# A new hand-written order for window attention with routed experts: all pieces re-ordered, sums and scores split in two float32r parts, masks loaded first, fewer idle products

## The chip, the cores and the metric

The program runs on one core of one Trainium2 chip. The number that counts is the device time of one execution in microseconds (us); lower is better. A core has five engines that run in parallel, each through its own list of instructions and strictly in that list's order: TensorE (PE, matrix products), VectorE (DVE), ScalarE (ACT), GpSimd (POOL) and SyncE (SP, which here only issues DMAs). They wait for each other through semaphores.

## The reference

Eight batches, each with eight attention heads over 576 positions and a head size of 64. Four heads look at a plain window of 32 positions, four at 32 positions with a step of 4. The attention result (576 x 512 per batch) goes through a routed expert: the 128 rows of each batch with the highest score get a two-layer product added.

```
scores = q @ k.T / 8                       # per batch and head, 576 x 576, masked to the window
attn   = softmax(scores)
x      = (attn @ v), heads side by side    # 8 x 576 x 512, float32
score  = x @ w_gate                        # 8 x 576
top    = the 128 rows of each batch with the highest score
out    = x, but out[top] = x[top] + sigmoid(score[top]) * (relu(x[top] @ w1) @ w2)
# w1: 512 x 1024, w2: 1024 x 512
```

## The kernel before, in words

**Pieces and their order.** The work is cut into some 1,100 pieces, and a table, `ORDER`, lists them. The program goes through the table once and issues the instructions of each piece on the engines that it uses, so the table fixes the order on every engine's list and in the DMA queues; there is no scheduler behind it. A piece is a letter code with its indices, `S 1 4` for batch 1, unit 4.

**Attention.** Each batch has five units `u` (0 and 1 hold the stepped heads, 2 and 3 the plain ones, 4 the rest of both). A unit runs through these pieces:
- `Q`, `K`, `VL`: DMAs that load queries, keys and values, nearly all on SP's queue. `ZP`, `ZV`, `ZA` spread loaded queries into a padded tile on POOL, DVE or ACT.
- `S` (lines 353 and 360): scores on PE; first a product of an identity with the mask tile `mk`, then 32 small products. `MX` (L367): row maximum on DVE. Then either `SU` (subtract on DVE) or `CS` (copy on ACT) and `SP2` (subtract on POOL).
- `TR` (L386): transposes on PE. `EX` (L395, L399): exponentials on ACT. `V` (L414): product with the values on PE.
- `DN`: divisors on DVE. `XM` (DVE, L435) or `XA` (ACT): the division. `ST`: store to the output by DMA.
- The gate score: either `GD` (product and sum on DVE, L471) or `GM` (product on POOL) and `GA` (sum on ACT).

**Routing, once a batch.** `RX` (`split_sums`, L481 to L492) splits six gate sums into three bfloat16 parts and spreads them by `blk`; `RO` (`in_order`, L502 and L504) brings them into row order by products on PE with the selection tiles `selw` and `sel_l`; `SC` adds the parts; `TP` splits the score into three bfloat16 parts on POOL; `SP` and `SB` make a row of it; `RK` (L530) and `RC` (L538) count the rank of each row; `RA`, `MV` (DVE) or `MK` (POOL) mark the rows with rank below 128; `PK` (L558) picks index and score by products; `IX`, `SG`, `SH` finish them, and `GT` gathers the 128 rows by an indirect DMA on POOL. `RO` and `PK` are exact because the parts add up to the float32 value.

**Experts.** `XT`, `XH`, `XL` turn the gathered rows and split them in a high and a low float32r part. Batches 1 and 2, 3 and 4, 5 and 6 share the first layer (`F`, L638, with `HH`, `HL`); batches 0 and 7 go alone (`N`, L654, `RL`, `HT`, `HI`, `HO`). `Y` (L679) is the second layer, `YO` (L684) the result and `SY` (L689) the indirect DMA that writes it back. There are 128 pieces `F`, `N` and `Y`, of six or three products each. The weights come by `LW` (DMA on SP's queue, two buffers), `WH` or `WV` (high part), `WL` (low part on POOL, which frees the buffer).

**The rest.** `C` pieces build constants: `C 0` issues the DMAs of the masks (`mraw`) and of the identity (`id32`) on POOL's queue, and `C 1` makes the bfloat16 identity `id16` (L191) and the first mask tile from them. `W n` (`idle`, L697) issues n products whose result nobody reads, so that PE has something to do; the program opens with `WARM` = 9 of them.

## Time and profile before

| | |
|---|---|
| device time, median of 3 runs | 284.77 us (283.71 to 286.86) |
| the profiled execution | 284.33 us, span 282.6 us |
| PE busy | 246.6 us, 87% of the span |
| DVE busy | 180.4 us, 64% |
| ACT busy | 146.2 us, 52% |
| POOL busy | 157.5 us, 56% |
| mean granted TensorE clock | 0.963 of full speed |
| moved by DMA | 53.15 MB |

The profiled execution is one run; its own time is 1.7 us longer than the span of its instructions. PE's busy time holds idle products and products at half clock too, so its 87% is more than the share of useful work.

### The profile page before, as it was taken

Reading aid. Unit: us, or ns where it says so; the run is one execution under the profiler, and the core shown is the slowest. Engines: PE = TensorE matmul, PEld = TensorE weight load, DVE = VectorE, ACT = ScalarE, POOL = GpSimd, SP = SyncE. Lnnn points to the kernel's source line nnn. Section 1 sums busy time; section 2 is a strip of 40 time slices with the busy share of each in tenths; the row PEclk is TensorE's granted clock in tenths of the full one; section 3 lists DMA queues with packets and bytes.
Section 4 is the critical chain, followed back from the end, with each engine's and each line's share of the span. In section 5 each row is a group of like instructions: output and inputs, shape, how many; then the busy total and the mean of one; then the engine's idle time right before and its main releaser. Section 6 shows DMA issues by size and latency. Waiting matters only on the chain.

```text
span 282.6 us, 8986 instructions
## 1 busy us (share of the span) xinstructions
PE 246.6 (87%) x3623; PEld 212.3 (75%) x3623; DVE 180.4 (64%) x491; ACT 146.2 (52%) x412; POOL 157.5 (56%) x206
## 2 busy tenths in 40 slices
...
GB/s 244 395 272 279 273 296 335 282 218 274 343 262 155 213 294 228 220 106 360 259 244 231 144 204 96 241 196 96 179 160 118 37 2 79 70 2 0 0 74 37
DMA packets 22489, 53.15 MB, mean 188 GB/s; under 512 B 2688, under 2 KB 13184, under 8 KB 21424
## 3 DMA queue, kind: packets, MB, share of 16 engines
...
## 4 chain that ended last, share of the span: by engine, by line
PE 38%; DVE 26%; issue 20%; DMA 6%; ACT 4%; POOL 3%; POOLq 1%; SPq 0%; DVEq 0%; ACTq 0%
PE a L414 9%; PE m L638 7%; PE s L360 6%; DVE rm L530 5%; PE m L679 5%; DVE junk L471 4%; PE m L386 3%; PE m L697 2%; DVE x L435 2%; DMA vl<-in_vb_dram 2%; DVE mx L367 2%; DMA id<-in_ident_dram 2%; PE s L353 2%; DVE rx L492 2%; DMA out_dram<-x 2%
## 5 line engine op out<-in xcount | busy, mean ns | idle before, releaser
L414 PEld LDWEIGHTS a<-v,pt 128*64 128x64 f32 x1152 | 42.8, 144 | 8.4 <-issue 5.7
L414 PE MATMUL a<-v,pt 128*64 128x65 f32 x1152 | 47.7, 230 | 1.5 <-DVE x L435 1.0
L360 PEld LDWEIGHTS s<-kq,zq 128*64 128x64 f32 x1216 | 44.7, 146 | 5.0 <-issue 2.2
L360 PE MATMUL s<-kq,zq 128*64 128x64 f32 (+2 forms) x1216 | 45.2, 230 | 1.4 <-issue 1.4
L463 POOL TENSOR_TENSOR gm<-x,wg 128x512 f32<-128x512 f32 x27 | 36.2, 1341 | 17.5 <-DVE x L435 5.4
L399 ACT ACTIVATE pt<-m 64x512 f32<-64x512 f32 x48 | 28.4, 592 | 24.3 <-PE a L414 12.4
L379 POOL TENSOR_TENSOR dt<-dt,mx 128x512 f32<-128x512 f32 x20 | 22.4, 1120 | 24.6 <-ACT dt L374 16.2
L367 DVE TENSOR_REDUCE mx<-s 128x8 f32<-128x512 f32 x40 | 27.0, 679 | 12.3 <-PE s L360 8.8
L395 ACT ACTIVATE pt<-m 32x256 f32<-32x256 f32 (+1 forms) x80 | 30.0, 375 | 9.0 <-PE m L386 8.1
L530 DVE SCALAR_TENSOR_TENSOR rm<-sb,ts,thr 128x576 bf16<-128x576 f32 (+3 forms) x32 | 29.1, 949 | 6.6 <-ACT sb L523 6.6
L307 POOL COPY zq<-kq 64x1152 f32<-64x1152 f32 (+1 forms) x25 | 30.2, 1209 | 4.0 <-DMA xe<-out_dram,ix 2.5
L689 POOL DMA_INDIRECT out_dram<-y,ix x8 | 8.0, 1001 | 39.9 <-DVE y L684 35.6
L638 PE MATMUL m<-xh,w1h 128*128 128x256 f32 x96 | 29.2, 304 | 0.7 <-ACT xh L620 0.7
L638 PE MATMUL m<-xl,w1h 128*128 128x256 f32 x96 | 27.8, 290 | 0.2 <-DVE xl L623 0.2
L638 PE MATMUL m<-xh,w1l 128*128 128x256 f32 x96 | 27.7, 289 | 0.0
L386 PE MATMUL m<-id,dt 128*128 128x128 f32 x160 | 25.6, 289 | 2.0 <-DVE dt L379 1.0
L679 PE MATMUL m<-w2h,hh 128*128 128x512 f32 x64 | 27.1, 423 | 0.0
L475 ACT ACTIVATE gm<-gm 128x256 f32<-128x256 f32 x54 | 22.2, 417 | 8.5 <-POOL gm L463 8.3
L679 PE MATMUL m<-w2h,hl 128*128 128x512 f32 x64 | 25.4, 396 | 0.0
L679 PE MATMUL m<-w2l,hh 128*128 128x512 f32 x64 | 25.3, 396 | 0.0
L353 PE MATMUL s<-mk,id 128*64 128x512 bf16 x80 | 16.4, 405 | 9.5 <-DVE mk L194 6.1
L433 ACT ACTIVATE x<-a,rin 128x64 f32<-128x64 f32 x88 | 19.2, 328 | 7.1 <-DVE rin L424 5.4
...
## 6 DMA issues: line engine op xcount, KB each, us to landing
...
raw<-in_w_dram SPq DMA_DIRECT2D x8, 512.0 KB, 6.2
...
```

The source lines that it names most:

```text
L307: copy(zqs[kind][r, :, lo:hi, h], src[r, :, G * lo:G * hi].rearrange("p g (t q) -> p g t q", q=G))
L360: nc.tensor.matmul(st[HB * g:HB * (g + 1), i, lo:hi], zqs[kind][:, g, t].rearrange("p h q -> p (h q)"), ks[b, kind][:, g, k0 + lo:k0 + hi] ...
L367: nc.vector.tensor_reduce(out=mx, in_=X["s", b, u], axis=AX.X, op=ALU.max)
L379: eng.tensor_tensor(out=dt, in0=st if eng is nc.vector else dt, in1=mx.unsqueeze(2).to_broadcast([P, 8, GK]), op=ALU.subtract)
L386: nc.tensor.transpose(tt[:, a * P:(a + 1) * P], dt[:, 2 * a:2 * a + 2].rearrange("p e k -> p (e k)"), id32)
L395: nc.scalar.activation(pt[o:o + n, y, e], tt[lo:lo + n, x].rearrange("k c (i q) -> k c i q", q=G), AF.Exp, scale=SCALE)
L399: nc.scalar.activation(pt[r, :, e], tt[r].rearrange("k (i q) -> k i q", q=G), AF.Exp, scale=SCALE)
L414: nc.tensor.matmul(av[r, a // 2, f], pt[:, i % 2, i // 2, a], values(b, u, a)[:, f], start=True, stop=True)
L463: nc.gpsimd.tensor_tensor(out=gm, in0=X["x", b, u], in1=gate_w(u), op=ALU.mult)
L530: nc.vector.scalar_tensor_tensor(out=out, in0=X["sb", b][:, t * P:S], scalar=ts[:, b, t:t + 1], in1=thr[:, 0:n], op0=ALU.subtract, op1=ALU ...
L638: nc.tensor.matmul(out, WS1[w][:, i, f * P:(f + 1) * P], X["x" + x, e][:, i, :], start=i == 0 and n == 0, stop=i == 3 and n == 2)
L679: nc.tensor.matmul(X["py", b], X["h" + x, e, c][:, o:o + P], WS2[w][:, i, :], start=i == 0 and k == 0, stop=i == 7 and k == 2)
```

## The change

**The table.** All pieces stand in a new order. The choice of engine changes with it: 27 units instead of 20 subtract on POOL (`CS`, `SP2`), 13 instead of 20 on DVE (`SU`); 21 gate sums instead of 13 run on DVE (`GD`), 19 instead of 27 on POOL and ACT (`GM`, `GA`); 36 divisions instead of 29 on DVE (`XM`), 4 instead of 11 on ACT (`XA`); 18 spreads of queries instead of 25 on POOL, 10 instead of 5 on ACT, 6 instead of 4 on DVE; 7 high parts of weights instead of 4 on ACT, 1 instead of 4 on DVE; 6 marks instead of 4 on DVE, 2 instead of 4 on POOL. The pairs of batches are the same.

**Splits.** `RX` makes two float32r parts instead of three bfloat16 parts: three DVE instructions a batch instead of eight. `TP` becomes two POOL instructions instead of four. The selection tiles and the marks become float32r, so `RO` (6 products a batch) and `PK` (5) run on float32r operands.

**Start.** The mask's DMA moves to ACT's queue, ahead of all else there; `id32` follows later on the same queue (`C 16`); `id16` is built on POOL without `id32`. The first scores are those of units 2 and 3.

**Idle products.** `W` issues 30 instead of 86, `WARM` 18 instead of 9.

```diff
-BUFS = dict(v0=1, v1=1, s=2, a=1, m=4, dt=2, x=3, gm=2, xe=3, xh=1, hh=3, raw=2, y=2, oh=1, sb=1, xl=1, hl=3, mx=3, den=3, rin=3, rx=2, g=8, ix=8, junkv=1, p3=2, rest=2, sm=2, restp=2)
-WARM = 9
+BUFS = dict(v0=1, v1=1, s=2, a=1, m=4, dt=2, x=3, gm=1, xe=3, xh=1, hh=3, raw=2, y=2, oh=1, sb=1, mx=4, rx=2, xl=1, hl=3, den=4, rin=4, g=8, ix=8, p2=2, sm=1)
+WARM = 18
...
-ZP 0 0 0, S 0 0, W 26, K 0 1 1, ZP 0 0 1, MX 0 0, CS 0 0, Q 0 1 1, C 14, C 2, Q 1 0, SP2 0 0, C 4, TR 0 0, VL 0 2,
...
+Q 1 1, K 1 1, VL 0 0, S 0 2, S 0 3, C 14, ZV 0 1 0 0, ZA 0 1 1 0, CS 0 2, C 13, DT 0 3, C 6, MX 0 2, MX 0 3, S 0 0,
...
-            nc.gpsimd.dma_start(out=mraw, in_=masks)
-            nc.gpsimd.dma_start(out=id32, in_=ident)
+            nc.scalar.dma_start(out=mraw, in_=masks)
...
-            nc.vector.memset(id16, 0.0)
+            nc.gpsimd.memset(id16, 0.0)
+            for h in range(2):
+                v = id16[0:G, G * h:G * (h + 1)]
+                nc.gpsimd.affine_select(out=v, in_=v, pattern=[[1, G]], compare_op=ALU.not_equal, fill=1.0, base=0, channel_multiplier=-1)
         elif i == 1:
-            nc.vector.tensor_copy(id16[0:G], id32[0:G, 0:G].unsqueeze(1).to_broadcast([G, 2, G]))
...
+        elif i == 16:
+            nc.scalar.dma_start(out=id32, in_=ident)
...
-        nc.sync.dma_start(out=qs[b, kind][:, :, lo:hi], in_=qt[b, kind].rearrange("p (h s) -> p h s", h=2)[:, :, lo:hi])
+        (nc.scalar if b == 0 and kind else nc.sync).dma_start(out=qs[b, kind][:, :, lo:hi], in_=qt[b, kind].rearrange("p (h s) -> p h s", h=2)[:, :, lo:hi])
...
-        (nc.scalar if b == 0 else nc.sync).dma_start(out=ks[b, kind][:, :, lo:hi], in_=kt[b, kind].rearrange("p (h s) -> p h s", h=2)[:, :, lo:hi])
+        nc.sync.dma_start(out=ks[b, kind][:, :, lo:hi], in_=kt[b, kind].rearrange("p (h s) -> p h s", h=2)[:, :, lo:hi])
...
-    def three(eng, out, x, rest):
-        eng.tensor_copy(out[0], x)
-        eng.tensor_tensor(out=rest, in0=x, in1=out[0], op=ALU.subtract)
-        eng.tensor_copy(out[1], rest)
-        eng.tensor_tensor(out=out[2], in0=rest, in1=out[1], op=ALU.subtract)
+    def two(eng, hi, lo, x):
+        eng.tensor_copy(hi, x)
+        eng.tensor_tensor(out=lo, in0=x, in1=hi.bitcast(F32), op=ALU.subtract)
 
 
     def split_sums(b):
-        X["p3", b] = p3 = new("p3", [P, 3, 6], f"p3_{b}", BF16)
-        X["rx", b] = rx = new("rx", [P, 4, 3, 4], f"rx_{b}", BF16)
-        three(nc.vector, [p3[:, i] for i in range(3)], gs[:, b, 0:6], new("rest", [P, 6], f"rest_{b}"))
+        X["p2", b] = p2 = new("p2", [P, 6, 2], f"p2_{b}", F32R)
+        X["rx", b] = rx = new("rx", [P, 4, 4, 2], f"rx_{b}", F32R)
+        two(nc.vector, p2[:, :, 0], p2[:, :, 1], gs[:, b, 0:6])
+        nc.vector.tensor_tensor(out=rx, in0=p2.bitcast(F32)[:, 0:4].unsqueeze(2).to_broadcast([P, 4, 4, 2]),
+                                in1=blk.unsqueeze(1).unsqueeze(3).to_broadcast([P, 4, 4, 2]), op=ALU.mult)
...
-        three(nc.gpsimd, [tk[:, b, :, 2 + i] for i in range(3)], ts[:, b], new("restp", [P, NTOK], f"restp_{b}"))
+        two(nc.gpsimd, tk[:, b, :, 2], tk[:, b, :, 3], ts[:, b])
...
-        X["oh", b] = oh = new("oh", [P, NTOK, P], f"oh_{b}_{s}", BF16)
+        X["oh", b] = oh = new("oh", [P, NTOK, P], f"oh_{b}_{s}", F32R)
...
-            nc.tensor.matmul(pi[:, 0:5], oh[:, t, :], tk[:, b, t, :], start=t == 0, stop=t == NTOK - 1)
+            nc.tensor.matmul(pi[:, 0:4], oh[:, t, :], tk[:, b, t, :], start=t == 0, stop=t == NTOK - 1)
```

**What the table moves, at three places.** First PE at the routing of batch 1. `a` is the result of `V`, `s` that of `S`, `m` a PSUM bank; before, the last rows ahead of `RO 1` on PE and `RO 1` itself:

```order
L386 MATMUL m_66<-id_75,dt_71 128x128 x4
L414 MATMUL a_1_1125<-v_0_844,pt_99 64x65 x16
L386 MATMUL m_67<-id_75,dt_70 128x128 x4
L617 MATMUL m_68<-id_75,xe_0_973 128x128 x4
L386 MATMUL m_69<-id_75,dt_71 128x128 x4
L414 MATMUL a_0_1178<-v_0_844,pt_98 64x65 x16
L502 LDWEIGHTS selw
L502 MATMUL m_66<-rx_1197,selw 128x3x4
```

The same engine and place with the change:

```order
L420 MATMUL a_2_951<-v_1_661,pt_99 64x65 x16
L699 LDWEIGHTS warm
L699 MATMUL m_67<-warm 128x256
L359 MATMUL s_3_990<-mk,id_76 64x512
L366 MATMUL s_3_990<-kq_90,zq_88 64x64 x16
L392 MATMUL m_69<-id_75,dt_71 128x128 x4
L619 MATMUL m_67<-id_75,xe_0_939 128x128 x4
L420 MATMUL a_3_1019<-v_1_661,pt_99 64x65 x16
L504 MATMUL m_68<-rx_984,selr 128x8 x4
L506 MATMUL m_68<-p_1_983,selr 128x2 x2
```

`RO 1` stood right behind the product that came before `RX 1` in the table (nothing of PE's lies between `RX 1` and `RO 1`); now a score unit of batch 1, a turn, the turn of the gathered rows and a `V` of batch 1 stand between the two.

Second DVE at the same routing, `RX 1`. `p` are the parts, `rx` the spread parts; before:

```order
L481 CAST p_1_1196<-gs 128x6
L482 TENSOR_TENSOR rest_1198<-gs,p_1_1196 128x6
L483 CAST p_1_1196<-rest_1198 128x6
L484 TENSOR_TENSOR p_1_1196<-rest_1198,p_1_1196 128x6
L492 TENSOR_TENSOR rx_1197<-p_1_1196,blk 128x12 x4
L423 TENSOR_SCALAR den_0_1221<-a_0_1178 128x8
```

And with the change:

```order
L604 CAST w1h<-raw_805 128x1024
L487 CAST p_1_983<-gs 128x6
L488 TENSOR_TENSOR p_1_983<-gs,p_1_983 128x6
L495 TENSOR_TENSOR rx_984<-p_1_983,blk 128x32
L625 TENSOR_TENSOR xl_1014<-m_67,xh_1013 128x4x128
```

Eight instructions became three, with one that reads `blk` instead of four.

Third DVE at the start of the program, where the first masks are made. `zq` are spread queries, `kq` loaded ones, `mk` the mask tiles; before:

```order
L189 MEMSET id_76 128x32
L191 CAST id_76<-id_75 32x64
L181 COPY mk<-mraw 128x512
L194 MEMSET mk 128x2x32
L181 COPY mk<-mraw 128x512
L198 MEMSET mk 128x32
L181 COPY mk<-mraw 128x512
L307 COPY zq_90<-kq_91 64x2x8x32
```

And with the change:

```order
L184 COPY mk<-mraw 128x512
L198 MEMSET mk 128x2x32
L313 COPY zq_88<-kq_90 64x36x32
L184 COPY mk<-mraw 128x512
L204 MEMSET mk 128x32
L184 COPY mk<-mraw 128x512
L313 COPY zq_89<-kq_92 64x2x8x32
L266 TENSOR_REDUCE blk<-id_75 128x4
L373 TENSOR_REDUCE mx_2_255<-s_2_194 128x8
```

The copy from `id_75` (`id32`) no longer stands ahead of the masks; the first read of `id_75` on DVE now stands behind them and ahead of the first row maximum.

## Rows read from the trace of the kernel before

**Rows 1.** The page, part 1: busy time, share and instructions of each engine.

```profile
PE 246.6 (87%) x3623; PEld 212.3 (75%) x3623; DVE 180.4 (64%) x491; ACT 146.2 (52%) x412; POOL 157.5 (56%) x206
```

**Rows 2.** Busy by stretch: length, PE, PEld, DVE, ACT, POOL, granted clock, DMA share, GB/s.

```profile
0.00:9.30 9.30, 2.11 (x11) 1.33 (x11) 4.06 (x9) 4.19 (x5) 8.03 (x15) 1.00 0.77 287
9.30:37.50 28.20, 25.68 (x470) 21.90 (x470) 13.53 (x33) 15.64 (x43) 19.34 (x49) 1.00 0.87 298
37.50:125.00 87.50, 71.14 (x1252) 60.55 (x1251) 76.19 (x190) 52.51 (x145) 63.26 (x60) 0.90 0.76 247
125.00:217.70 92.70, 89.99 (x1557) 79.12 (x1555) 69.22 (x218) 63.10 (x196) 52.58 (x64) 1.00 0.62 198
217.70:277.20 59.50, 57.63 (x342) 49.39 (x340) 16.66 (x43) 10.75 (x25) 13.32 (x21) 0.97 0.09 32
277.20:282.60 5.40, 0.00 (x0) 0.00 (x0) 0.75 (x1) 0.00 (x0) 0.96 (x1) 0.94 0.13 49
```

**Rows 3.** The same view of the stretches with a low granted clock.

```profile
45.00:50.00 5.00, 3.45 (x43) 2.97 (x43) 3.43 (x11) 1.79 (x5) 2.55 (x6) 0.66 0.96 363
75.00:82.50 7.50, 5.38 (x106) 4.95 (x106) 5.39 (x18) 2.17 (x4) 2.83 (x6) 0.77 0.86 288
92.50:100.00 7.50, 6.07 (x91) 5.12 (x92) 7.22 (x27) 4.91 (x9) 3.78 (x4) 0.77 0.69 247
102.50:110.00 7.50, 6.90 (x116) 6.38 (x117) 5.38 (x14) 3.76 (x13) 4.33 (x8) 0.77 0.83 263
120.00:125.00 5.00, 3.90 (x44) 3.26 (x44) 3.77 (x16) 3.95 (x11) 4.48 (x7) 0.66 0.19 63
240.00:245.00 5.00, 4.78 (x28) 4.63 (x27) 0.32 (x1) 0.00 (x0) 0.72 (x1) 0.66 0.30 105
```

**Rows 4.** Waits: who waited for whom, total us, times, longest us.

```profile
PE m L502 <- DVE rx L492: 7.8, 4, 3.3
...
PE s L353 <- DVE mk L194: 6.1, 1, 6.1
...
PE m L538 <- DVE rm L530: 2.5, 4, 1.0
```

**Rows 5.** Timeline of `RX 1` and `RO 1`: start, duration, instruction, idle before.

```profile
73.62 2.34 POOL L606 TENSOR_TENSOR w2l<-raw,w2h 128x1024 fp32r<-128x1024 f32 x1
...
73.71 2.52 DVE L492 TENSOR_TENSOR rx<-p,blk 128x12 bf16<-128x12 bf16 x4
...
76.04 0.41 PE L502 MATMUL m<-rx,selw 128*128 128x12 bf16 x4 [3.30 <-DVE rx L492]
```

**Rows 6.** The chain of waits: start, us on the chain, what.

```profile
12.82 4.37 PE m L697 x26
17.18 0.44 PE m L386 x4
...
29.41 2.40 PE m L697 x22
...
185.28 2.80 PE m L679 x12
```

**Rows 7.** Timeline of the start.

```profile
7.88 0.97 DVE L191 CAST id<-id 32x64 bf16<-32x64 f32 x1 [3.63 <-DMA id<-in_ident_dram]
...
9.29 0.64 PE L353 MATMUL s<-mk,id 128*64 128x512 bf16 x2 [6.07 <-DVE mk L194]
```

**Rows 8.** Idle products (L697) and gate sums on DVE (L471): min/median/max ns, first and last start.

```profile
L697 PE MATMUL m<-warm x95: 269/273/422, 1.1 to 64.4; 128*128 128x256 bf16 x95
...
L471 DVE CUSTOM_DVE_ANT_0 junk<-x,wg x26: 414/426/1848, 38.4 to 212.9; 128x256 bf16<-128x256 f32 x26
```

**Rows 9.** DMA issues of the weights: count, KB each, median us to landing.

```profile
raw<-in_w_dram SPq DMA_DIRECT2D x8, 512.0 KB, 6.2
```

**Rows 10.** Timeline of PE late in the program.

```profile
216.58 1.15 PE L414 MATMUL a<-v,pt 128*64 128x65 f32 x32
...
229.66 0.39 PE L538 MATMUL m<-neg,rm 128*128 128x1 bf16 x10
```

More of the change, by code (lines that the diff above doesn't have):

```diff
@@ L144, in tile_window_attention_moe @@
     id32 = cp.tile([P, P], F32, name="id32")
-    id16 = cp.tile([P, 2, G], BF16, name="id16")
-    mraw = cp.tile([P, 2 * GK], BF16, name="mraw")
+    id16 = cp.tile([P, 2 * G], BF16, name="id16")
+    mraw = new("hl", [P, 512], "mraw", F32R).bitcast(BF16)[:, 0:2 * GK]
     mk = cp.tile([P, 4, 8, GK], BF16, name="mk")
     wg = cp.tile([P, 3, 256], F32, name="wg")
-    selw = cp.tile([P, P + 3], BF16, name="selw")
-    sel_l = cp.tile([P, 2, P], BF16, name="sel_l")
+    selr = cp.tile([P, 2 * (P + 2) + 2 * P], F32R, name="selr")
+    selw, sel_l = selr[:, 0:2 * (P + 2)].rearrange("p (c m) -> p c m", c=2), selr[:, 2 * (P + 2):].rearrange("p (c m) -> p c m", c=2)
     blk = cp.tile([P, 4], F32, name="blk")
@@ L167, in tile_window_attention_moe @@
     ts = cp.tile([P, B, NTOK], F32, name="ts")
-    tk = cp.tile([P, B, NTOK, 5], BF16, name="tk")
+    tk = cp.tile([P, B, NTOK, 4], F32R, name="tk")
+    tk32 = cp.tile([P, NTOK, 2], F32, name="tk32")
     gs = cp.tile([P, B, 11], F32, name="gs")
@@ L173, in tile_window_attention_moe @@
     warm = cp.tile([P, 256], BF16, name="warm")
+    X = {}
     def clear_q():
@@ L224, in constants @@
         elif i == 4:
-            nc.gpsimd.tensor_copy(tk[:, :, :, 0], toks32[:, 0:1].unsqueeze(2).to_broadcast([P, B, NTOK]))
-            for t in range(NTOK):
-                nc.gpsimd.memset(tk[:, :, t, 1], float(t * P))
+            nc.gpsimd.tensor_copy(tk32[:, :, 0], toks32[:, 0:1].to_broadcast([P, NTOK]))
+            nc.gpsimd.tensor_tensor(out=tk32[:, :, 1], in0=toks32, in1=tk32[:, :, 0], op=ALU.subtract)
+            nc.gpsimd.tensor_copy(tk[:, :, :, 0:2], tk32.unsqueeze(1).to_broadcast([P, B, NTOK, 2]))
             nc.gpsimd.memset(gs[:, :, 10], 0.0)
```

170 lines of the change are left out of this document (83 added, 87 removed).

## The prediction

> **What bounds the kernel now.** I read the busy table first [rows 1]: PE has 87% of the span, the next engine (DVE) 64%. So the question is what PE's time is made of, and when it stands still. By stretch [rows 2] there are three regimes. Up to 9.3 us nothing useful runs on PE. From 37.5 to 125 us PE is busy 71.14 of 87.5 us while DVE is busy 76.19, and the granted clock is 0.90: here PE waits for chains that run through DVE. From 125 us on PE is busy 97% and all else has slack, until the last 5.4 us, in which only the last result is written. So time is to be won before 125 us and in what PE does there; work that is merely moved within the last 150 us wins nothing.
>
> I split the span of 282.6 us into six parts, all seen from PE:
> - A, until the first useful product: 9.3 us [rows 7].
> - B, after the last product: 5.4 us [rows 2].
> - C, waits in between: PE is idle for 282.6 - 246.6 = 36.0 us; of this 5.4 lie at the end, and of the first 9.3 us 2.1 are busy, so 7.2 lie in A. C is 23.4 us. 7.8 of it are four waits of `RO` for `RX`, 2.5 four waits of `RC` for `RK` [rows 4].
> - D, idle products inside: `W` issues 86. The 26 near the start took 4.37 us (168 ns each, some at half rate), 22 later ones 2.40 (109 ns each) [rows 6]; the other 38 at 109 ns make 4.1. D is 10.9 us.
> - E, loss to the clock: six stretches [rows 3] in which a part ran at 1.2 instead of 2.4 GHz, each behind waits of PE. (1 - 0.66) x 5.0 or (1 - 0.77) x 7.5 is 1.7 us each time. E is 10.2 us.
> - F, the rest, useful work at the clock of the rest of the run: 282.6 - 59.2 = 223.4 us.
>
> **The change, part by part.**
>
> *Start.* Today the first score waits 6.07 us for the mask tile, and that for `id32`, whose copy DVE awaits for 3.63 us until 7.88 [rows 7]. With the change neither stands ahead of the first score; what does is the landing of `Q 0 0` and `K 0 0`, 2 x 576 KB. In A the DMA engines moved 287 GB/s on average [rows 2], nothing in the first two microseconds; these two and the 0.4 MB on the other queues then need until about 7 us, a spread and two mask copies on DVE about 1.5. I take A = 8.5, with 7.5 and 11 as ends (11 if loads land as slowly as the median weight load, 6.2 us [rows 9], one behind the other in part). More counts what follows: today PE fills 12.82 to 17.18 us with 26 idle products while the one scored unit goes through DVE, ACT and POOL [rows 6]; then three units can be scored by then. The 18 opening products end near 5 us, under the loads, and cost nothing. The row maxima stand behind a read of `id32` on DVE, now issued near 5 us; it should land by 10.5, when the first maximum is due. If not, DVE is late by the difference, 1 to 2 us, and all of batch 0 behind it.
>
> *RX and RO.* The four waits are order, not work: before, PE has 0 to 1.0 us of products between `RX` and `RO` in all eight batches (I counted the pieces in between, a unit of `S` 1.3, `V` 1.0, `TR` 0.4 us). With the change it is 1.7 to 8.3 us (batch 0 to 7: 3.9, 3.2, 2.1, 8.3, 2.1, 6.9, 4.4, 1.7). And the chain itself loses five of its eight DVE instructions. The worst wait, 3.30 us, came when four of them took 2.52 us beside a POOL instruction of 2.34 [rows 5]; now two can be caught there, not six. I take the 7.8 us as gone. The Trainium skill (SBUF — State Buffer, Who interferes with whom) says that a VectorE instruction with two SBUF inputs and a GpSimd instruction that reads SBUF exclude each other for a whole instruction; rows 5 agree.
>
> *Marks, ranks, picks.* `SP` to `RC`, which holds `RK`, has 4.5 to 15.6 us of PE work between them (before 4.5 to 13.0), so half of the 2.5 us goes. `PK` to `XT`, which holds the gather, has at least 5.6 us.
>
> *float32r.* `RO` and `PK` are 11 products a batch, 88 in all. Ten bfloat16 products with 128 columns of weights pass in 0.39 us with the last one's latency, so under 40 ns each [rows 10]; four float32 ones, which also stream 128 columns, take 0.44 us on the chain, 110 ns each [rows 6]. Here 2 to 8 columns are streamed. The ends are 0 and +70 ns; I take +50, that is +4.4 us (0 to +6.2). It falls on F. The skill (TensorE: Matmul & The Clock Gate, Weight-path perf modes) speaks against this part: fast weight loads need a type other than FP32. If that holds for float32r, 128 columns at its 1.2 columns per ns are 107 ns, an estimate of 9.4 us for the 88; no row shows such a product alone.
>
> *Engine choice.* DVE gets 8 more gate sums (a pair of 0.43 us at the median), 7 more divisions and 2 more marks, and loses 7 subtractions, 3 weight copies and 40 small instructions of `RX`: about level. POOL loses some 20 us, ACT some 10. Nothing of this is on PE's list; it decides how long chains are. The gate sums are two-input instructions, 414 ns at best and 1848 when caught [rows 8], so more of them on DVE can also make it later.
>
> *Expert pieces.* By the last attention product (`V 7 2`, at 216.6 us today [rows 10]) the list has 55 of 128 pieces `F`, `N`, `Y` behind it, with the change 87. So 32 x 0.7 us (three products of 0.233 [rows 6]) move into the stretch in which PE waits. They save nothing by themselves, F holds them anyhow, but they are what PE runs under the chains of DVE, so they are why C can shrink. What they cost: the tail has fewer fillers. Behind `V 7 2` stand 41 pieces and the routing of batch 7, some 32 us of PE work; the chain of batch 7 up to its gather takes about 16 us, and its second half is covered except for one turn (`HT 7 1` behind `RL 7 1`, one `Y` in between): 1 us.
>
> *Idle products.* 30 x 109 ns is D = 3.3. Some of the 7.6 us come back as waits, since `W` stands where PE has nothing else: I put half, 3.8 us, into C.
>
> *Queue.* `LW 6`, `LW 4` and `LW 5` now stand on SP's queue ahead of `VL 2 0` and `VL 2 1`, and each waits for a `WL` on POOL (2.34 us [rows 5]). From the `WL` that frees `LW 5` to `V 2 4` PE has 5.8 us of work, and a weight load takes 6.2 us [rows 9], with a second one and the values behind it. I put 3.5 us into C. Stores are not late by this: each division has at least 6 us of work behind the store that frees its buffer.
>
> *The sum.* C: 23.4 - 7.8 - 2.5 leaves 13.1 of small waits, mostly of turns and scores for DVE. The pieces between `S` and `TR` grow from a median near 5 to near 8 us, so I halve them: 6.5. With 3.8, 3.5 and the tail's 1.0 that is 14.8. E: three of the six low stretches follow a wait for `RX` (45, 75 and 120 us); they go, E = 5.1. The span is 8.5 + 5.4 + 14.8 + 3.3 + 5.1 + 223.4 + 4.4 = 264.9 us. The profiled execution took 1.7 us more than its span, 284.33, and the median of the runs is 284.77, so I add 1.7 and no more: **267 us**.
>
> **Rivals.**
> - *It fits better still.* With 32 pieces more to fill with, C falls to 8 and E to 1.7, float32r costs nothing: 264.9 - 6.8 - 3.4 - 4.4 = 250.3, so 252 us. For it: from 125 us on, with fillers, PE waits only 2.7 of 92.7 us [rows 2]. Against it: there DVE had 25% slack; with the change PE and DVE both fill the stretch.
> - *The waits come back elsewhere.* DVE is busy 87% from 37.5 to 125 us [rows 2] and its work does not shrink, so PE may wait as long for other pieces: C stays 23.4, E 10.2. 264.9 + 8.6 + 5.1 = 278.6, so 280 us. For it: the gate sums caught by POOL, and the weights on SP's queue. Against it: the counted cover, longer at nearly every kind of chain.
> - *Slower: the clock stays low early.* All of `W` starts before 65 us [rows 8], and only one low stretch lies there [rows 3]. With two thirds gone, PE has gaps between 10 and 60 us, where some 37 us of useful work stand, and half clock doubles what runs in it. It turns the sign once it adds 18.1 us, half of this work; at two thirds, 25 us, the time is 292. Against it: PE has the same scores to do there and starts them earlier.
>
> **How the numbers follow.** Forecast 0.62 (its own range 260 to 274: A's ends, float32r's ends, C by 4 either way), better still 0.12, waits come back 0.19 (274 to 286), clock 0.07. 8 times in 10: 255 to 280. A difference under 1% (282 to 287.6) can hardly be told from none. Faster by over 1%: 0.62 + 0.12 + 0.12 = 0.86; within: 0.06; slower: 0.08.
>
> **What would show it.** PE busy near 241 us of a span near 265. The wait of `RO` for `RX` under 2 us in all. No idle gap of 3 us on PE after the start. Three or fewer low stretches. The first score product at 8 to 9 us. `V 7 2` at 218 to 230 us, and from there some 37 us to the end. `RO`'s and `PK`'s products over 60 ns apart. A wait of PE or ACT near `V 2 4` or `WH 5`. I am wrong if DVE's chains, not PE's list, pace the stretch behind 60 us: then PE shows many short waits for row maxima and subtractions, and E does not fall.

## The result and the profile after

The changed kernel takes **267.9 us** (median of 4 runs, 264.89 to 268.17) against 285.5 us (4 runs, 283.71 to 286.86) of the kernel before on the same chip: ratio 0.936, 95% interval 0.928 to 0.945. The forecast was 267, the range 255 to 280. Here and in the table below, medians are over all runs, while ratios and intervals leave out runs over 1.5% above the fastest of their kernel, and with only two runs left there is no interval. The profiled execution has a span of 265.8 us; the sum in the prediction gave 264.9.

The busy line of the changed kernel, from its page (against [rows 1]):

```profile
PE 243.0 (91%) x3576; PEld 212.3 (80%) x3576; DVE 185.0 (70%) x481; ACT 139.3 (52%) x340; POOL 138.4 (52%) x174
```

Busy time by stretch, cut where the first useful product starts, at the old 37.5 and 125 us, behind the last attention product and behind the last product (against [rows 2]):

```profile
0.00:6.50 6.50, 4.02 (x18) 2.68 (x19) 4.09 (x10) 4.72 (x5) 5.29 (x18) 1.00 0.64 239
6.50:37.50 31.00, 26.75 (x564) 22.90 (x563) 25.68 (x55) 17.15 (x40) 24.76 (x46) 1.00 0.95 331
37.50:125.00 87.50, 79.83 (x1232) 69.99 (x1233) 69.11 (x171) 54.06 (x122) 50.10 (x43) 0.90 0.75 244
125.00:227.80 102.80, 99.79 (x1576) 89.27 (x1574) 73.08 (x211) 57.51 (x161) 52.89 (x60) 0.98 0.54 175
227.80:260.40 32.60, 32.56 (x190) 27.47 (x189) 12.32 (x39) 5.89 (x14) 4.35 (x6) 1.00 0.15 53
260.40:265.80 5.40, 0.03 (x1) 0.00 (x0) 0.75 (x1) 0.00 (x0) 0.97 (x1) 0.70 0.13 49
```

Between 37.5 and 125 us PE is now busy 79.8 of 87.5 us instead of 71.1, and DVE 69.1 instead of 76.2: the stretch that waited for DVE became PE's. At the end PE has next to no gap (busy 32.56 of 32.60 us). The price is seen in the fourth line: the last attention product ends at 227.8 us, 10 us later than before, and only 38 us follow it instead of 65.

The stretches with a low granted clock (against [rows 3]), the longest waits of PE (against [rows 4]), and a wait of the kernel before that [rows 4] leaves out:

```profile
45.00:60.00 15.00, 12.50 (x183) 10.39 (x182) 11.72 (x31) 7.31 (x19) 8.79 (x6) 0.66 0.58 179
62.50:72.50 10.00, 7.42 (x24) 6.14 (x25) 7.06 (x15) 3.10 (x8) 7.79 (x9) 0.66 0.71 196
135.00:140.00 5.00, 4.54 (x74) 3.99 (x76) 1.96 (x5) 2.58 (x9) 3.95 (x7) 0.66 0.60 170
```

```profile
PE m L392 <- POOL dt L385: 5.2, 4, 2.0
PE m L504 <- DVE rx L495: 2.9, 2, 2.6
PE s L359 <- DVE mk L204: 1.4, 1, 1.4
PE a L420 <- DVE rk L544: 1.3, 1, 1.3
PE m L540 <- DVE rm L532: 1.1, 1, 1.1
```

```profile
PE m L386 <- DVE dt L379: 1.0, 3, 0.4
```

Three low stretches instead of six, but longer ones: (1 - 0.66) x 30 us is 10.2 us, as much as before. `RO` waits 2.9 us for `RX` instead of 7.8. The largest wait is a new one: the turns (L392) for a subtraction on POOL (L385), 5.2 us in four pieces, three of them before 31 us; in the kernel before the turns waited 1.0 us for subtractions, on DVE.

Nearly all that is left of the wait of `RO` is one place, batch 1. Timeline: start, duration, instruction, idle time before it:

```profile
61.65 2.34 POOL L608 TENSOR_TENSOR w1l<-raw,w1h 128x1024 fp32r<-128x1024 f32 x1
61.75 2.27 DVE L488 TENSOR_TENSOR p<-gs,p 128x6 fp32r<-128x6 f32 x1
...
64.05 0.97 DVE L495 TENSOR_TENSOR rx<-p,blk 128x32 fp32r<-128x32 f32 x1
...
65.08 1.01 PE L504 MATMUL m<-rx,selr 128*128 128x8 f32 x4 [2.63 <-DVE rx L495]
```

This is [rows 5] again: a subtraction of six columns took 2.27 us because it stood beside the same kind of POOL instruction, and ended 0.03 us behind it. In `new_order_gd_first` below, where no such instruction stands beside it, it takes 0.17 us.

### The profile page after: what moved, and what is told of

Its sections match the earlier page's. It is cut to its first block, busy times and chain, and to the rows that moved or that the text cites. A ratio compares the mean times of both kernels' runs of the same rounds, so it can differ in the third digit from the quotient of the medians.

```text
span 265.8 us, 8759 instructions
## 1 busy us (share of the span) xinstructions
PE 243.0 (91%) x3576; PEld 212.3 (80%) x3576; DVE 185.0 (70%) x481; ACT 139.3 (52%) x340; POOL 138.4 (52%) x174
## 4 chain that ended last, share of the span: by engine, by line
PE 61%; DVE 17%; POOL 7%; issue 6%; ACT 5%; DMA 2%; POOLq 1%; DVEq 0%; ACTq 0%
PE m L640 12%; PE m L681 12%; PE a L420 12%; PE s L366 7%; PE m L392 5%; PE m L656 5%; DVE mx L373 2%; DVE x L441 2%; DVE warm L477 2%; DVE rm L532 2%; DMA out_dram<-y,ix 2%; PE s L359 2%; POOL dt L385 2%; PE m L560 2%; PE m L520 1%
## 5 line engine op out<-in xcount | busy, mean ns | idle before, releaser
L366 PEld LDWEIGHTS s<-kq,zq 128*64 128x64 f32 x1216 | 45.6, 148 | 3.2 <-issue 0.4
L469 POOL TENSOR_TENSOR gm<-x,wg 128x512 f32<-128x512 f32 x19 | 27.1, 1426 | 28.6 <-DVE x L441 10.7
L385 POOL TENSOR_TENSOR dt<-dt,mx 128x512 f32<-128x512 f32 x27 | 28.9, 1075 | 21.6 <-ACT dt L380 15.3
L392 PE MATMUL m<-id,dt 128*128 128x128 f32 x160 | 25.3, 284 | 5.7 <-POOL dt L385 5.2
L313 POOL COPY zq<-kq 64x1024 f32<-64x1024 f32 (+1 forms) x18 | 20.3, 1128 | 19.0 <-DMA kq<-in_qt_dram 13.6
L640 PE MATMUL m<-xh,w1h 128*128 128x256 f32 x96 | 28.1, 293 | 0.0
L477 DVE CUSTOM_DVE_ANT_0 warm<-x,wg 128x256 bf16<-128x256 f32 x42 | 26.9, 641 | 1.0
L380 ACT COPY dt<-s 128x512 f32<-128x512 f32 x27 | 15.6, 587 | 22.3 <-DVE den L429 6.3
L532 DVE SCALAR_TENSOR_TENSOR rm<-sb,ts,thr 128x576 bf16<-128x576 f32 (+3 forms) x32 | 23.2, 772 | 5.4 <-ACT sb L525 5.2
L392 PEld LDWEIGHTS m<-id,dt 128*128 128x128 f32 x160 | 18.0, 142 | 10.4 <-POOL dt L385 7.4
L441 DVE TENSOR_TENSOR x<-a,rin 128x512 f32<-128x512 f32 x36 | 24.9, 691 | 1.9
```

What stands on the lines that cost most here:

```text
L366: nc.tensor.matmul(st[HB * g:HB * (g + 1), i, lo:hi], zqs[kind][:, g, t].rearrange("p h q -> p (h q)"), ks[b, kind][:, g, k0 + lo:k0 + hi] ...
L385: eng.tensor_tensor(out=dt, in0=st if eng is nc.vector else dt, in1=mx.unsqueeze(2).to_broadcast([P, 8, GK]), op=ALU.subtract)
L392: nc.tensor.transpose(tt[:, a * P:(a + 1) * P], dt[:, 2 * a:2 * a + 2].rearrange("p e k -> p (e k)"), id32)
L441: nc.vector.tensor_tensor(out=xv, in0=av[:, :, :, 0:D], in1=rin.unsqueeze(3).to_broadcast([P, 2, 4, D]), op=ALU.mult)
L477: nc.vector.tensor_tensor_reduce(out=warm, in0=X["x", b, u][:, c], in1=gate_w(u)[:, c], scale=UP, scalar=0.0, op0=ALU.mult, op1=ALU.add, a ...
L532: nc.vector.scalar_tensor_tensor(out=out, in0=X["sb", b][:, t * P:S], scalar=ts[:, b, t:t + 1], in1=thr[:, 0:n], op0=ALU.subtract, op1=ALU ...
```

## The experiments

"Before" is the kernel before, run with them on the same chip. The times of one chip stand together.

| run | us, median | before, us | ratio (95%) |
|---|---|---|---|
| the change | 267.9 | 285.5 | 0.936 (0.928 to 0.945) |
| new_order_bf16 | 272.0 | 286.0 | 0.955 (0.945 to 0.964) |
| old_order_w30 | 281.1 | 286.0 | 0.983 (0.974 to 0.992) |
| old_order_start | 283.1 | 286.0 | no interval |
| new_order_pool_moved | 261.9 | 286.0 | 0.915 (0.906 to 0.925) |
| new_order_ro_close | 284.3 | 282.7 | 1.007 (1.002 to 1.011) |
| new_order_w0 | 270.0 | 282.7 | no interval |
| new_pool_w (one run) | 265.2 | 282.7 | no interval |
| new_order_fixed | 264.1 | 282.7 | 0.937 (0.933 to 0.941) |
| new_order_again | 269.5 | 282.8 | 0.951 (0.945 to 0.957) |
| new_order_pool_again | 266.7 | 282.8 | 0.944 (0.939 to 0.949) |
| new_order_gd_first | 264.4 | 282.8 | 0.938 (0.932 to 0.944) |
| old_order_ro_late | 287.4 | 282.8 | 1.009 (1.005 to 1.014) |

**The new order with the old splits.**

```diff
-        two(nc.vector, p2[:, :, 0], p2[:, :, 1], gs[:, b, 0:6])
+        three(nc.vector, [p3[:, i] for i in range(3)], gs[:, b, 0:6], new("rest", [P, 6], f"rest_{b}"))
...
-            nc.tensor.matmul(pi[:, 0:4], oh[:, t, :], tk[:, b, t, :], start=t == 0, stop=t == NTOK - 1)
+            nc.tensor.matmul(pi[:, 0:5], oh[:, t, :], tk[:, b, t, :], start=t == 0, stop=t == NTOK - 1)
```

> The new order and start with the old splits: eight VectorE instructions in each RX, four on GpSimd in each TP, RO and PK with three bfloat16 parts. Theory (the float32r products cost PE time, and the cover behind RX, not its shorter chain, took the waits away): in the trace of the changed kernel a batch pays 0.24 us for the four products of RO, 0.17 for the two others and 0.33 for PK, about 0.75 us; eight batches 6 us, of which some five lie where PE is bound. So 262 to 265 us, and the waits of RO for RX stay under 4 us in all. Rival (the shorter chain was needed): the eight instructions bring the waits back, at least 5 us more of them, and the time is 270 us or above.

272.0 us: the theory's time was wrong. Its part on the products holds, its part on the waits does not. First the products. `RO` (L504, L506) and `PK` (L560) of the changed kernel at full clock:

```profile
128.18 0.51 PE L504 MATMUL m<-rx,selr 128*128 128x8 f32 x4
128.54 0.36 PE L506 MATMUL m<-p,selr 128*128 128x2 f32 x2
...
210.46 0.61 PE L560 MATMUL m<-tk,oh 128*128 128x4 f32 x5
```

The same three in this kernel:

```profile
208.11 0.26 PE L505 MATMUL m<-rx,selw 128*128 128x12 bf16 x4
208.22 0.19 PE L507 MATMUL m<-p,sel_l 128*128 128x3 bf16 x2
215.54 0.28 PE L561 MATMUL m<-tk,oh 128*128 128x5 bf16 x5
```

The differences are 0.25, 0.17 and 0.33 us, 0.75 us a batch and 6.0 in all, 68 ns for each of the 88 products. PE's busy time says the same: 235.3 us here against 243.0, and 1.7 of the 7.7 us are clock. So float32r costs PE what the theory said. But part of the waits came back:

```profile
PE m L505 <- DVE rx L495: 6.0, 3, 4.0
```

6.0 us instead of 2.9, 3.1 more, where the rival asked for 5. And the start was worse for a reason that nobody had in mind. The start of this kernel:

```profile
4.68 3.49 POOL L213 MEMSET pt<- 128x1024 f32 x3
...
4.96 0.82 DVE L181 COPY mk<-mraw 128x512 bf16<-128x512 bf16 x1 [0.74 <-DMA mraw<-in_masks_dram]
...
7.20 1.11 DVE L181 COPY mk<-mraw 128x512 bf16<-128x512 bf16 x1
...
8.52 0.64 PE L356 MATMUL s<-mk,id 128*64 128x512 bf16 x2 [3.38 <-DVE mk L201]
```

The same place in the changed kernel:

```profile
4.95 0.29 DVE L184 COPY mk<-mraw 128x512 bf16<-128x512 bf16 x1 [0.73 <-DMA mraw<-in_masks_dram]
...
5.96 0.38 DVE L184 COPY mk<-mraw 128x512 bf16<-128x512 bf16 x1
...
6.55 0.64 PE L359 MATMUL s<-mk,id 128*64 128x512 bf16 x2 [1.41 <-DVE mk L204]
6.55 3.06 POOL L216 MEMSET pt<- 128x1024 f32 x3
```

The bfloat16 selection tile takes POOL less time to make, so its clearing of `pt` starts at 4.68 instead of 6.55 us, beside the mask copies on DVE, and stretches them from 0.29 and 0.38 to 0.82 and 1.11 us: the first product comes 2.0 us later. Taken from that product on, the two kernels need 253.9 and 255.2 us. So, from the first product on, the splits are worth about 1.3 us in these two executions, one of each kernel. Up to the 20th attention unit they win 3.7 us (111.9 against 115.6 us), where chains through DVE pace. Behind it they lose 2.4 us (142.0 against 139.6): five batches of 0.75 us and a low stretch of 1.7 us, which only the changed kernel has there, less 3.0 us of waits that only this kernel has (1.2, 1.3 and 0.5 us at 143, 158 and 207 us).

**Fewer idle products in the old order.** `W 26, 10, 22, 5, 4, 12, 7` became `W 6, 4, 7, 3, 3, 4, 3`.

> The old order with 30 idle products instead of 86 (26, 10, 22, 5, 4, 12, 7 become 6, 4, 7, 3, 3, 4, 3). Theory (prediction's step): 56 products of 109 ns are 6.1 us, the 20 at the start cost up to 168 ns, and half comes back as waits: 281 to 283 us. First rival (W stood only where PE had nothing to do): 284 to 286 us, the waits grow by what W shrinks. Second rival (the clock stays low early): two or more low stretches more before 65 us and 288 us or above.

281.1 us, 5.0 less (0.8 to 2.6%). The busy line of its page:

```profile
PE 239.3 (85%) x3567; PEld 205.6 (73%) x3567; DVE 179.4 (64%) x491; ACT 146.4 (52%) x412; POOL 158.5 (57%) x206
```

In the profiled executions PE's busy time falls by 7.3 us, 1.7 of it clock, and its idle time grows from 36.0 to 40.7 us: of 5.6 us of idle products 4.7 came back as waits. These two executions differ by 2.6 us (0.9 from the products, 1.7 clock), the medians by 5.0; how the other 2.4 divide between waits and clock stays open. No low stretch was added before 65 us, so the second rival falls.

**No idle product in the new order.** All nine `W` are taken out of the table.

> The changed kernel without the 30 idle products of W (the 18 opening ones stay). Theory (prediction's step, half comes back): 3.3 us go, 1.6 come back, 266 to 267 us. Rival (they stand only where PE waits anyway): 267 to 269, PE's busy time 3.3 us less and its idle time 3.3 us more. Second rival (they hold the clock up): a new stretch at 1.2 GHz before 45 us and 270 us or above.

270.0 us, against 267.9 and 269.5 us of the changed kernel on two chips. Its busy line and its largest wait:

```profile
PE 238.0 (89%) x3546; PEld 208.6 (78%) x3546; DVE 187.8 (70%) x481; ACT 139.5 (52%) x340; POOL 138.6 (52%) x174
```

```profile
PE m L396 <- POOL dt L389: 8.3, 6, 3.1
```

PE's busy time falls by 5.0 us (1.7 of it clock) and its idle time grows from 22.8 to 29.6, 6.8 us for some 3.2 us of products; the waits for subtractions on POOL alone grow from 5.2 to 8.3 us. So the theory is out: the 30 products stand where PE waits anyway, and cost nothing. The signs of the second rival are there too, a median of 270.0 us and a new low stretch before 45 us:

```profile
27.50:35.00 7.50, 5.78 (x97) 4.96 (x98) 7.14 (x15) 4.88 (x11) 5.23 (x5) 0.77 0.88 292
```

But this stretch is 1.7 us, the clock as a whole costs less here than in the change (8.5 against 10.2 us), and the repeat of the changed kernel (`new_order_again`), which has all its `W`, shows a low stretch at the same place. So the runs don't show that these 30 products hold the clock up.

**The start in the old order.**

```diff
-            nc.gpsimd.dma_start(out=mraw, in_=masks)
-            nc.gpsimd.dma_start(out=id32, in_=ident)
+            nc.scalar.dma_start(out=mraw, in_=masks)
...
-K 0 1 0, C 15,
+K 0 1 0, C 16, C 15,
```

> The old order with the new start alone: the mask's DMA first on ACT's queue, id16 built on GpSimd, the identity later on ACT's queue. Theory: the first score product starts at 6.5 to 7.5 us instead of 9.3, and the whole moves by as much: 282 to 283 us. Rival (the first tenth is paced by loads and by the one scored unit's way through three engines): the first product is earlier, but TR of that unit and all behind it are not, 284 to 286 us.

283.1 against 286.0 us. The first product starts at 5.84 instead of 9.29 us, the fifth attention unit ends 4.5 us earlier (32.8 against 37.3), the 37th 5.9 us (198.3 against 204.2), the last product only 2.0 us (275.2 against 277.2). What takes the rest back in this execution is one load of values that landed late, and a low stretch of 1.7 us behind it:

```profile
204.59 0.24 PE L416 MATMUL a<-v,pt 128*64 128x65 f32 x1 [2.27 <-DMA v<-in_va_dram]
```

The kernel before has no such wait. So the theory holds: the earlier start reaches the attention units in full and more, and its rival (the units are not earlier) is out. How much of it reaches the end hangs on that load: the four runs go from 278.8 to 284.2 us.

**RO close behind RX in the new order.**

```diff
-GD 0 4, RX 0, EX 1 0, CS 1 2, TR 1 1,
-S 1 4, VL 1 1, V 1 0, EX 1 1, S 1 3, MX 1 4, DN 1 0, ZP 2 1 0, RO 0,
+GD 0 4, RX 0, RO 0, EX 1 0, CS 1 2, TR 1 1,
+S 1 4, VL 1 1, V 1 0, EX 1 1, S 1 3, MX 1 4, DN 1 0, ZP 2 1 0,
...
```

> The changed kernel with RO moved right behind RX in its table, as far as the PSUM banks allow: at once in batches 0, 1, 2, 4 and 7, one piece later in 6, nine later instead of 28 in 5, unchanged in 3. RX keeps its three instructions. Theory (cover took the waits away): PE waits 1 to 3 us in at least five batches for RX and for the gate sums ahead of it, 6 to 10 us in all instead of 2.9, with one or two low stretches more: 273 to 279 us. Rival (the shorter chain was enough): waits under 4 us in all, 267 to 270 us.

284.3 us: the whole gain is gone, more than the theory asked for. Its wait of PE for `RX`, and the four low stretches:

```profile
PE m L509 <- DVE rx L500: 12.7, 5, 6.3
```

```profile
32.50:42.50 10.00, 7.69 (x99) 6.92 (x97) 4.98 (x14) 4.08 (x9) 3.29 (x4) 0.50 0.93 330
52.50:60.00 7.50, 7.17 (x98) 6.22 (x100) 4.76 (x13) 3.03 (x7) 6.10 (x5) 0.54 0.53 151
65.00:75.00 10.00, 6.25 (x81) 5.69 (x82) 4.14 (x4) 1.13 (x4) 5.03 (x5) 0.66 0.66 212
210.00:217.50 7.50, 7.50 (x129) 7.09 (x129) 2.97 (x12) 0.64 (x2) 0.00 (x0) 0.57 0.26 84
```

Its span (282.3) is 16.5 us longer: PE's idle time grows by 13.7 us, 9.8 of them for `RX`, and its busy time by 2.8 us. The clock's share, reckoned as above, grows by 4.9 us (15.1 against 10.2), but part of it falls on the waits, so it can't be added to them. 6.3 us of the 12.7 are `RX 1`. Its subtraction is held by POOL as long here as in the change and in `new_order_bf16` (2.26, 2.27 and 2.27 us), while PE waits 6.3, 2.6 and 4.0 us for it: the collision is there each time, and what stands between `RX` and `RO` decides what PE feels of it.

**RO later in the old order.** `RO` stands one to three units of PE work further back, `SC` a little later in three batches.

```diff
-RX 1, ST 1 4, RO 1, XH 0, GM 2 1, DN 2 0, XM 2 0, S 3 1, K 3 0, SC 1, WL 4, GA 2 1, GD 2 0,
+RX 1, ST 1 4, XH 0, GM 2 1, DN 2 0, XM 2 0, S 3 1, RO 1, K 3 0, WL 4, GA 2 1, GD 2 0, SC 1,
...
```

> The kernel before with RO moved later in its table, behind one to three units of PE work more (1.3 to 2.5 us), and SC a little later in batches 0, 1 and 4. Everything else stays, the eight instructions of RX too. Theory (the four waits are order, not work): they fall from 7.8 us to 3 us or less, with one or two of the three low stretches behind them: 277 to 281 us. Rival (the chain through VectorE sets the pace, PE waits as long one piece later): 283 to 286 us.

287.4 us, by the ratio slower by 0.5 to 1.4%: the rival. The waits of PE that changed:

```profile
PE a L419 <- DVE x L440: 3.3, 2, 2.6
PE s L358 <- DVE dt L384: 3.0, 2, 1.6
...
PE m L391 <- DVE dt L384: 2.8, 3, 2.1
...
PE m L507 <- DVE rx L497: 2.2, 1, 2.2
```

The wait for `RX` fell by 5.6 us, from 7.8 to 2.2, as expected. The three waits above it, for divisions and subtractions of DVE, were 4.4 us together in the kernel before and are 9.1 here, and 2.2 us more went to a load of values that landed late, as in `old_order_start`. The clock costs 10.2 us as before.

**Two places of POOL's list.**

```diff
-WH 0, DN 1 2, XM 1 2, WV 1, EX 2 1, RX 1,
+WH 0, WH 1, DN 1 2, XM 1 2, EX 2 1, RX 1,
...
-N 0 1 0, N 0 0 0, GM 1 2, WL 1, N 0 1 1,
+N 0 1 0, N 0 0 0, WL 1, GM 1 2, N 0 1 1,
...
-SY 0, F 1 2 3, ZP 5 0 1, SB 3, SP2 4 2,
+SY 0, F 1 2 3, SB 3, SP2 4 2, ZP 5 0 1,
```

> The changed kernel with two places of GpSimd's list altered. First, the high part of weight 1 goes to ACT right behind that of weight 0, and its low part ahead of GM 1 2, so that it should run near 57 us and not beside RX 1. Second, ZP 5 0 1, which stood behind the scatter SY 0 and started 4.47 us late, goes behind the subtraction SP2 4 2, for which PE waited 1.97 us at 135 us. Theory (a VectorE instruction of two SBUF inputs is held for the whole GpSimd instruction beside it; each wait of 2 us also costs a stretch at 1.2 GHz): RO waits under 0.4 us for RX 1, TR 4 2 under 0.4 us, the low stretches 62.5 to 72.5 and 135 to 140 us are gone; 2.3 + 3.4 + 1.6 + 1.7 = 9 us at most, so 258 to 263 us. Rival (DVE's chains pace the stretch, and PE waits as long at the next chain): idle time of PE between 37.5 and 125 us stays at 7 us or more, 265 to 268 us.

261.9 us against 286.0, the best ratio of all. A second run on another chip gave less:

> A second look at the kernel of new_order_pool_moved, beside the next two on the same chip: 260 to 263 us.

265.2 us (one run), and with the changed kernel beside it on one chip:

> new_order_pool_moved once more: 260 to 263 us; if it is 265 to 266, its gain over the changed kernel is 1 to 2 us only and most of what the two removed waits gave came back.

> The changed kernel once more, on the chip of the next two: 266 to 269 us, and in its trace again the waits of 1.1 to 2.6 us at 47, 49, 65 and 135 us, each with a stretch at 1.2 GHz behind it.

266.7 against 269.5 us; by the ratios (0.944 and 0.951) 0.7% less, and their intervals overlap, so the gain is small and not clear of the noise. The repeat of the changed kernel shows all that was expected of it: waits of 1.1, 1.3, 2.6 and 1.9 us that end at 47, 49, 66 and 136 us, and low stretches behind them; it has two more low stretches, of 1.7 us each, at 7 and 31 us. In all three profiled executions of the altered kernel the wait for `RX 1` is gone, and each time two others stand there: 1.3 to 2.0 us at 61 us, where two idle products wait for a gate sum (L477) that the two weights' low parts on POOL now hold, and 1.5 to 2.1 us at 134 us for `ZP 5 0 1` itself. So for the waits the rival is right. The clock differs most between the three: by the same reckoning 3.4, 8.5 and 6.8 us are lost to it, in one program. It does not order them alone: the spans are 260.8, 263.5 and 265.5 us, and PE's idle time is 22.3, 23.3 and 24.4 us.

**Four more edits, and one moved gate sum.** Against the kernel of `new_order_pool_moved`; `WC` issues idle products that read constants.

```diff
-DN 0 1, XM 0 1, GD 0 1, ST 0 1, EX 0 0, V 0 0, VL 1 0, Q 2 1, MX 1 0, CS 1 0, DN 0 0,
+DN 0 1, XM 0 1, MX 1 0, GD 0 1, ST 0 1, EX 0 0, V 0 0, VL 1 0, Q 2 1, CS 1 0, DN 0 0,
...
-XM 1 1, RC 0, GA 1 0, V 1 4,
+XM 1 1, WC 12, RC 0, WC 10, GA 1 0, V 1 4,
...
-XM 1 4, MX 2 4, SP2 2 0, DT 2 4, GD 1 4, V 1 2, W 2, SU 2 4,
+XM 1 4, GD 1 4, MX 2 4, SP2 2 0, DT 2 4, V 1 2, SU 2 4,
...
-SY 0, F 1 2 3, SB 3, SP2 4 2, ZP 5 0 1,
+ZP 5 0 1, SY 0, F 1 2 3, SB 3, SP2 4 2,
```

> new_order_pool_moved with four more edits: 12 idle products ahead of RC 0 and 10 ahead of V 1 4, which read constants; the two idle products behind V 1 2 taken out (in new_order_pool_moved they waited 1.98 us at 61 us for a gate sum on VectorE, which uses the tile they read as scrap space); ZP 5 0 1 ahead of the scatter SY 0 (PE waited 1.58 us for it at 134 us); the maximum MX 1 0 ahead of GD 0 1 (PE waited 1.51 us at 31 us for its unit). Theory: the waits of 1.1 and 1.3 us at 48 to 50 us caused the stretch at 1.2 GHz from 50 to 57 us, which goes (3.5 us), and the three other waits go too (5.1 us less what returns, half): 253 to 257 us, no low stretch but at most one. Rival for the clock (idle products don't hold it): the stretch stays, 257 to 260 us. Rival for the waits (the next chain on VectorE takes their place): idle time of PE between 7 and 150 us stays at 11 us or more, 258 to 261 us.

> new_order_fixed with one piece moved on VectorE's list: the gate sum GD 1 4 goes ahead of MX 2 4, so that it runs at 53 us, beside the gather, and not beside SP2 2 0 and two low parts of weights, where its first half took 5.79 us instead of 0.41 and PE waited 5.14 us behind it. Theory (the instruction is shut out as long as GpSimd goes from one instruction to the next without a break): both halves take under 0.5 us, the 5.14 us and the stretch at 1.2 GHz from 57 to 65 us go, 8.5 us less at most, 255 to 258 us. Rival (another VectorE instruction of two SBUF inputs is caught in its place, that is RX 1): a wait of 2 us or more for RX 1, 259 to 262 us.

(`new_order_fixed` has all of it but the move of `GD 1 4`.) 264.1 and 264.4 us, both above their forecasts (253 to 257 and 255 to 258). The clock part held in both: the stretch from 45 to 57.5 us in `new_order_gd_first`:

```profile
45.00:57.50 12.50, 8.89 (x167) 7.47 (x166) 12.11 (x20) 8.34 (x19) 10.21 (x7) 1.00 0.56 168
```

and in `new_order_pool_again`, without the idle products:

```profile
45.00:57.50 12.50, 10.01 (x124) 8.51 (x121) 9.66 (x23) 5.96 (x14) 9.21 (x8) 0.61 0.55 174
```

1.00 against 0.61. (PE's lower busy time in the first is the beginning of the next wait, from 54 us on, of which more below.) In the six profiled executions of the new order in which PE waits at these two places (the change and its repeat, the three of the altered kernel, `new_order_w0`) a low stretch begins between 47.5 and 50.3 us; in the two with idle products there none begins between 45 and 57.5 us. So idle products in the two waits kept the clock up. The waits at 31 us (1.5) and 134 us (`ZP` now ahead of the scatter, 0.4 left) went too. The rival for the waits holds in `new_order_fixed` even so: between 7 and 150 us PE is idle 12.6 us. The move of the gate sum failed. Timeline of `new_order_gd_first`:

```profile
50.94 1.07 POOL L584 DMA_INDIRECT xe<-out_dram,ix  x1 [0.15 <-issue]
...
51.41 6.56 DVE L477 CUSTOM_DVE_ANT_0 warm<-x,wg 128x256 bf16<-128x256 f32 x1
52.03 1.06 POOL L385 TENSOR_TENSOR dt<-dt,mx 128x512 f32<-128x512 f32 x1
...
53.03 4.65 POOL L608 TENSOR_TENSOR w1l<-raw,w1h 128x1024 fp32r<-128x1024 f32 x2
...
59.93 0.64 PE L359 MATMUL s<-mk,id 128*64 128x512 bf16 x2 [5.94 <-DVE dt L385]
```

One half of a gate sum, 0.42 us elsewhere, took 6.56 us: it started beside the gather and ended only behind the subtraction and both low parts of weights, which ran without a break until 57.68. In `new_order_fixed` it was 5.79 us, in `new_order_pool_moved` 4.47. So a gate sum can be held for a whole run of POOL instructions, as the theory said, and my remedy failed. Neither is so everywhere. In the changed kernel a half that starts at 84.83 us beside a subtraction ends at 86.09, behind the first of two subtractions (84.77 to 86.99 us without a break). And in the kernel before a half runs its normal time beside a gather:

```profile
60.58 1.08 POOL L582 DMA_INDIRECT xe<-out_dram,ix  x1 [5.78 <-DMA raw<-in_w_dram]
61.09 0.42 DVE L471 CUSTOM_DVE_ANT_0 junk<-x,wg 128x256 bf16<-128x256 f32 x1
```

Why the one in `new_order_gd_first` did not end within the gather's time stays open. The maxima and subtractions queued behind on DVE then cost PE 5.94 us and the next low stretch, from 57.5 to 65 us. Even so this is the kernel with the lowest median on its chip, 264.4 us against 269.5 of the changed kernel.

## Why the prediction was right, point by point

The total was right within 1 us, but partly by luck: the clock cost 5.1 us more than forecast and float32r 1.6, the start 2.0 less and the rest 3.8 less. The core of the mechanism was right as far as it was tried: PE's idle time between 37.5 and 125 us falls from 16.4 to 7.7 us, and with `RO` moved back close behind `RX` the whole gain is gone.

| part | predicted, us | measured, us |
|---|---|---|
| A, until the first useful product | 8.5 | 6.55 |
| B, after the last | 5.4 | 5.4 |
| C, waits in between | 14.8 | 22.8 idle - 2.5 in A - 5.4 in B = 14.9 |
| D, idle products | 3.3 | 3.2 (PE busy without them: 4.95 less, 1.7 of it clock) |
| E, clock | 5.1 | 10.2 |
| float32r | 4.4 | 6.0 |
| F, the rest | 223.4 | 219.6 (what is left of 265.8) |

- **Start.** Too late by 2.0 us, outside its ends (7.5 to 11). The step that failed is the landing of the first loads at "about 7 us": ACT and DVE already spread them at 4.85 and 5.35 us. Nor are the loads what the first product waits for last: it waits 1.41 us for the mask tile, as in the kernel before. That it counts at the end was right in sign: alone in the old order it gave 2.9 us in the medians, and 5.9 us in the trace until a late load took most of it back.
- **RX and RO.** "I take the 7.8 us as gone" was too good: 2.9 stay, 2.63 of them in the very collision of [rows 5], which the step held possible and priced at nothing. As to what took the waits away: with cover and eight instructions they are 6.0 us, with three instructions and hardly any cover 12.7, with both 2.9, in one profiled execution each. Cover weighs more, and the shorter chain another 3.1 us. But cover for `RO` alone in the old order only moves the waits. What the new order has is cover at nearly all chains at once; that this makes the difference, and that it is due to the 32 expert pieces moved forward was argued and not tried.
- **Waits in sum.** 14.9 against 14.8, by luck in its parts: the 3.5 us for weights on SP's queue never appear (no wait of PE over 0.35 us between 66 and 102 us; a weight load landed in 4.8 us at the median, not in the 6.2 us that the step used), nor does the tail's 1.0 us; in their place stand the 2.9 us at `RO` and the 5.2 us of turns for POOL's subtractions, which the step had only as part of its halved rest. Seven more units subtract on POOL, and the prediction counted POOL's load but not that PE would wait for it. Of the 5.2 us, 1.97 are the spread `ZP 5 0 1` behind a scatter, as the moved spread showed; for the rest the seven units are the likely cause, which was not tried.
- **Clock.** The step "three of the six low stretches go" was right in number and wrong in price: not 1.7 us each but 5.1, 3.4 and 1.7. The sign that the prediction had named for this, that E does not fall, came true: E is 10.2 us as before, though between 66 and 102 us PE does not wait for DVE. That idle products in place of waits prevent a low stretch is shown at 45 to 57.5 us. Not every wait starts one: behind a wait of 1.5 us that ends at 30 us the change has none, and its repeat has one. How long it then lasts is not in the order alone, as the three executions of one program show.
- **Idle products.** "Half comes back" was right for the old order's sign (4.7 of 5.6 us in the traces) and wrong for the 30 that stayed: without them PE waits longer by more than they took.
- **float32r.** The mechanism was right and the size near its upper end, 68 instead of 50 ns a product. The Trainium skill (TensorE: Matmul & The Clock Gate, Weight-path perf modes) excludes FP32 weights from fast weight loads; the runs agree that float32r does not load fast either: at full clock the starts of these products lie mostly 111 to 112 ns apart, those of the bfloat16 ones 25 to 28, some more at the first of a group. The 9.4 us that the prediction estimated from it and the measured 6.0 are not the same thing: 9.4 counts 107 ns for each product as a whole, which is near the 112, and 6.0 is what each costs above a bfloat16 product. The trade is nearly even: the splits are worth some 1.3 us in the two executions compared.
- **Rivals.** "It fits better still" is out: C is 14.9 us and not 8, and float32r costs 6.0. The clock rival is out: no low stretch lies before 45 us in the change, and the two in its repeat (at 7 and 31 us) are 3.4 us together, where it asked for 18. "The waits come back elsewhere" describes two experiments (`old_order_ro_late`, `new_order_pool_again`), but not the change.
- **What stays open.** F is 3.8 us below the forecast, and no run tells why; as a remainder it also takes up what the other parts count twice or miss. Had it come out as forecast, the span would have been 4.7 us longer than predicted.

The signs that were named: PE busy 243.0 of 265.8 us (named near 241 of 265); no idle gap of 3 us; three low stretches; `V 7 2` at 226.7 us and 38 us from its end on; `RO` and `PK` products 60 ns and more apart: all as said. The wait of `RO` under 2 us, the first product at 8 to 9 us and a wait near `V 2 4` or `WH 5`: not as said. Of the signs of being wrong, that E does not fall came, many short waits behind 60 us did not.
